# Half-array units in pairs, PSUM banks handed out by modelled free time, late loads on GpSimd, in a fused spectral filter and gated MLP

## The chip, the cores and the metric

The kernel runs on one core of one Trainium2 chip. The metric is the device time of one execution in microseconds (us), lower is better. A core has TensorE (PE, matrix products), VectorE (DVE), ScalarE (ACT), GpSimd (POOL) and SyncE (SP, which here only issues DMAs). PSUM, into which TensorE writes, is used as eight banks of 512 float32 columns on 128 partitions.

## The reference

```python
def _A_ref(x, w_r, w_i):                 # x: 1 x 2048 x 512
    X = jnp.fft.rfft2(x.astype(jnp.float32), axes=(-2, -1))
    X = X * (w_r + 1j * w_i)             # weights 2048 x 257
    return jnp.fft.irfft2(X, s=(S, D), axes=(-2, -1)).astype(jnp.bfloat16)

def _B_ref(x, w_gate, w_up, w_down):     # 512 x 1792, 512 x 1792, 1792 x 512
    h = _gelu(x @ w_gate) * (x @ w_up)
    return h @ w_down

x = A_x
xn = _layernorm(x, axis=-1)
return x + _A_ref(xn, A_w_r, A_w_i) + _B_ref(xn, B_w_gate, B_w_up, B_w_down)
```

Two branches work on the same normalised rows: a two-dimensional Fourier transform with a filter and its inverse, and a gated MLP. Both are added to the input.

## The kernel before

**The MLP branch** is the backbone. The 2048 rows are four blocks b of 512. For each of 14 chunks fc of the hidden width, `gate` multiplies (four matmuls of 512 columns), ScalarE applies gelu into one of two `gl` buffers, `up` multiplies (four matmuls), and VectorE multiplies the two into `hT`. A `down` for one tile of 128 rows is 14 matmuls over all chunks, in three parts of 5, 5 and 4. The downs of a block stand among the gates and ups of the next block, after fc 2, 5, 8 and 11; the last block's four downs come at the end.

**The Fourier branch** runs as small units between these. In the forward part, `trans` transposes normalised rows into `xnT`, `butter` folds them on VectorE, `unit_D(j)` transforms along the width for row tile j (16 of them) into `xs`, and `unit_A(j)` does the first stage along the sequence into `tt`. Each `tt` tile is stored to a scratch tensor in HBM and loaded back in another order as `tv`. `load_tv(j - 1)` is issued right behind the store of tile j. `unit_B(h)` needs all 16 `tv` loads; it does the second stage, and VectorE multiplies by the filter (`mul`, four operations with `Wr` and `Wi`) into `yy`. `unit_C(h)` begins the inverse; its results go through a second scratch tensor and come back as `vv`, laid in the arena that held the forward constants. `unit_row`, which needs all of `vv`, `unit_E(j)` and `unit_F(j)` finish the inverse; the last sum is stored to the output.

D, E, F, gate, up and down use the whole 128 x 128 array. A, B and C use half of it per matmul: A and C contract over 64 partitions, two row halves side by side, and B writes 64 output partitions, two column halves side by side. Each has four matmuls of about 257 columns.

**The order** is written by hand. After each gate, each up and each part of a down stands a `hook`, numbered from 0; `at(h, ...)` puts units at hook h. Block 0 has hooks 0 to 27 and each later block 40, because of its downs. Work that `mul` and the final sums leave for VectorE waits in `later` until the next `flush`: at a hook after an up or a part of a down it is flushed at that hook, and at a hook after a gate it waits until the up's product has been issued. TensorE takes all of it in this order.

**Banks** are fixed: gate 0, up 1 and 2 in turn, D and E 3 and 4, A, C (a pair of banks) and F 5 and 6, B 3 and 4, trans and down 7.

**Queues.** The first loads (x, the MLP weights, the forward constants) are issued by SP and ScalarE at the start. The late loads (`wd` at hooks 10 to 16, `be` at 18, four loads of `Wr` and `Wi` at 19 to 28, `cm` at 31 and 34, `gm` at 52) are issued by SP through `load_late`, each with a wait for the TensorE work before its hook. SP also issues all scratch stores and loads in program order. GpSimd computes `rstd` for each chunk of four row tiles (chunks 1 to 3 at hooks 3, 13 and 23; the normalisation that needs it is three and four hooks later), and copies one row per E unit.

**The start.** `warm(24)` runs 24 matmuls on a zeroed tile `dumm` to get TensorE going. ScalarE writes one column of the same `dumm` with a gelu, which loads its table.

The class `_Prog` records every operation with the keys it reads and writes and derives the semaphore waits. Lines of use in the profile: 283 is every ordinary DMA, 287 a late load, 305 the first gelu, 324 the warm-up, 330 to 342 the normalisation, 351 trans, 391 to 394 D, 415 and 419 A, 425 the eviction to `tt`, 439 B, 445 its eviction, 451 to 454 the filter's products, 465 C, 471 its eviction, 484 the row, 498 E, 524 to 527 F, 559 gate, 562 gelu, 572 up, 575 the product `hT`, 585 down, 596 the sum behind a down.

Of the kernel before, what the change touches and what calls it, by code (L numbers as in the profile page):

```python
# [7 lines left out]
ACT = mybir.ActivationFunctionType  # L8
# [3 lines left out]
F32 = mybir.dt.float32  # L12
# [5 lines left out]
P = 128  # L18
# [91 lines left out]
class _Prog:  # L110
# [17 lines left out]
    def op(self, eng, fn, r=(), w=(), dma=False, after=()):  # L128
        deps = [(ev, True) for ev in after]
        for k in r:  # L130
            if k in self.writer:
                deps.append((self.writer[k], True))
        for k in w:
            if k in self.writer:
                deps.append((self.writer[k], False))
            for ev in self.readers.get(k, ()):
                deps.append((ev, False))
        need = {}
        for (st, val), raw in deps:
            if st == eng and not dma and (eng == "pe" or not raw):  # L140
                continue
            need[st] = max(need.get(st, 0), val)
        known = self.known[eng]
        need = {s: v for s, v in need.items() if known.get(s, 0) < v}
        need = {s: v for s, v in need.items()
                if not any(s2 != s and self.clk[(s2, v2)].get(s, 0) >= v for s2, v2 in need.items())}
        for s, v in need.items():
            for a, b in self.clk[(s, v)].items():
                if known.get(a, 0) < b:
                    known[a] = b  # L150
        if dma:
            st = next((d for d in self.dsem if known.get(d, 0) >= self.cnt[d]), None)
            if st is None:
                st = "d%d" % len(self.dsem)
                self.sem[st] = self.es.enter_context(self.nc.semaphore("s_" + st))
                self.cnt[st] = 0
                self.dsem.append(st)
# [33 lines left out]
def bass_parallel_sum__spectral_gfnet__glu_gated_geglu__prompt_kernel(  # L191
# [26 lines left out]
    with ExitStack() as es:  # L218
# [46 lines left out]
        mhalf = sb("mhalf", [P, 4], F32)  # L265
        rstd = sb("rstd", [P, NJ], F32)
        dumm = sb("dumm", [P, 512], F16)

        psum = es.enter_context(nc.psum_tensor("ps", [P, 8 * 512], F32))
        psum_h = psum[:, :].bitcast(F16)  # L270
# [8 lines left out]
            return psum[:, i * 512:(i + 2) * 512].rearrange("p (a c) -> p a c", a=2)[:, :, 0:KD]  # L279


        def dma(eng, dst, src, r=(), w=()):
            return op(eng, lambda e: e.dma_start(dst, src), r=r, w=w, dma=True)  # L283

        def load_late(dst, src, keys):

            op("sp", lambda e: e.dma_start(dst, src), w=keys, dma=True, after=[("pe", pr.cnt["pe"])])
# [17 lines left out]
        op("act", lambda e: e.activation(dumm[:, 0:1], mhalf[:, 0:1], ACT.Gelu_apprx_tanh), r=["mhalf"], w=["dumm"])  # L305
        dma("sp", fd[:], c_fd.ap(), w=["fd"])
        load_w(wg_sb, wgv, "wg", 2, 6, "sp")
        load_w(wu_sb, wuv, "wu", 2, 6, "sp")
# [33 lines left out]
            op("dve", lambda e: e.tensor_scalar(xn[:, j % 4, :], x_sb[:, j, :], ag[:, j, 0:1], rstd[:, j:j + 1], ALU.subtract, ALU.mult),  # L342
               r=[("x", j, 0), ("x", j, 1), ("ag", j), ("rstd", j)], w=[("xn", j % 4)])

        def trans(m, dcs, jjs, bk, eng="dve"):
            def f(e):
                ins = None
                for a, dc in enumerate(dcs):
                    for c, jj in enumerate(jjs):
                        i = a * len(jjs) + c  # L350
                        ins = e.transpose(bank_h(bk)[:, i * P:(i + 1) * P], xn[:, jj, dc * P:(dc + 1) * P], ident[:])  # L351
# [28 lines left out]
        later = []  # L380

        def unit_D(j):
            bk = 3 + j % 2
            m = j // 4
            f = fold[m % 2]
            k = ("fold", m % 2)
# [20 lines left out]
                w=[("vv", h)] + (AKEYS if h == 0 else []))  # L407

        def unit_A(j):
            bk = 5  # L410
            x4 = xs[j % 4]

            def fn(e):
# [16 lines left out]
                load_tv(j)  # L430

        def unit_B(h):
            bk = 3

            def fn(e):
                ins = None
# [18 lines left out]
            later.append(mul)  # L455

        def unit_C(h):
            bk = 5
            y = yy[h % 4]

            def fn(e):
# [18 lines left out]

        def unit_row():

            bk = 3
            op("pe", lambda e: e.matmul(bank(bk)[0:32, 0:64], vv[:, :, 256], EMs[:, 0:64], start=True, stop=True,
                                        skip_group_check=True), r=["be"] + VALL, w=[("ps", bk)])
            op("act", lambda e: e.activation(row[:], bank(bk)[0:32, 0:64], ACT.Copy, scale=SC_E), r=[("ps", bk)], w=["row"])
# [1 line left out]
                r=["row"], w=["z256"] + [("xn", i) for i in range(4)])  # L488

        def unit_E(j):  # L490
            bk = 3 + j % 2

            def fn(e):
                o = bank(bk).rearrange("p (c r b q) -> p c b r q", c=2, r=2, b=2)
# [22 lines left out]
                dma("sp", ov[b, :, j, :], osb[k][64 * b:64 * b + 64, :], r=[("osb", k)], w=[("out", j, b)])  # L517

        def unit_F(j):
            bk = 5 + j % 2  # L520

            def fn(e):
                z = zt[j % NZ]
# [27 lines left out]

        def gate(b, fc):
            k = gun[0]
            bg = 0

            def fn(e):
                ins = None
# [18 lines left out]

        def down(b, jj):
            j = 4 * b + jj
            bk = 7

            def part(f0, f1):
                def fn(e):
                    ins = None
                    for fc in range(f0, f1):
                        ins = e.matmul(bank(bk), hT[b % 2][:, fc, jj * P:(jj + 1) * P], wd_sb[:, fc, :], start=(fc == 0), stop=(fc == NFC - 1))  # L585
# [5 lines left out]
            part(5, 10)  # L591
            hook()
            part(10, 14)

            def add(dst, key):
                op("dve", lambda e: e.tensor_tensor(dst, bank(bk), x_sb[:, j, :], ALU.add), r=[("ps", bk), ("acc", j), ("x", j, 0), ("x", j, 1)], w=[key])  # L596
# [37 lines left out]
        for m in range(1, 4):  # L634
# [6 lines left out]
            at(a + 8, (trans, m, (0, 1), (0, 1, 2, 3), 7))  # L641
            at(a + 9, (trans, m, (2, 3), (0, 1, 2, 3), 7))
# [12 lines left out]
        for j in range(NJ):  # L655
            at(101 + 3 * j, (unit_E, j))
# [8 lines left out]
            ln_norm(2 * i)  # L665
            ln_norm(2 * i + 1)
        for i in range(2):
            trans(0, (0, 1), (2 * i, 2 * i + 1), 3 + 2 * i, "dve")
            trans(0, (2, 3), (2 * i, 2 * i + 1), 4 + 2 * i, "act")
        for b in range(4):  # L670
            for fc in range(NFC):
                gate(b, fc)
# [60 lines left out]
```

## Time and profile before

| what | us |
|---|---|
| median of 3 runs | 230.37 (229.06 to 230.85) |
| the profiled execution | 228.33 |
| its span, first to last instruction | 226.5 |
| TensorE busy | 198.8 (88%) |
| VectorE busy | 113.2 (50%) |
| ScalarE busy | 89.4 (39%) |
| GpSimd busy | 9.3 (4%) |
| first gate starts | 14.26 |
| first unit of stage B starts | 87.36 |
| the row unit starts | 154.57 |
| last down ends, about | 222.7 |

In the profile's busy slices one digit stands for one fortieth of the span, 5.66 us, and gives the busy share in tenths. In a timeline row stand start, duration, engine, line and operation; rows of several instructions are merged and end with the count, and the bracket says how long the engine had been idle and what ended that. In the chain of work that ended last, a row has start, duration and what it was. In a list of waits stand the engine and line that waited, what it waited for, the total, the number of times and the longest. In a row of the costliest groups stand the count, then the busy time in us and the mean duration in ns. A row of DMA issues has the count, the size of each and the median us from issue to landing.

### The profile page before, as it was taken

Reading aid. Unit: us, or ns where it says so; the run is one execution under the profiler, and the core shown is the slowest. Engines: PE = TensorE matmul, PEld = TensorE weight load, DVE = VectorE, ACT = ScalarE, POOL = GpSimd, SP = SyncE. Lnnn points to the kernel's source line nnn. Section 1 sums busy time; section 2 is a strip of 40 time slices with the busy share of each in tenths; the row PEclk is TensorE's granted clock in tenths of the full one; section 3 lists DMA queues with packets and bytes.
Section 4 is the critical chain, followed back from the end, with each engine's and each line's share of the span. In section 5 each row is a group of like instructions: output and inputs, shape, how many; then the busy total and the mean of one; then the engine's idle time right before and its main releaser. Section 6 shows DMA issues by size and latency. Waiting matters only on the chain.

```text
span 226.5 us, 3103 instructions
## 1 busy us (share of the span) xinstructions
PE 198.8 (88%) x1145; PEld 89.4 (39%) x1145; DVE 113.2 (50%) x262; ACT 89.4 (39%) x157; POOL 9.3 (4%) x26
## 2 busy tenths in 40 slices
PE   1989898999976805999999999997999999999883
PEld 0344444445422302333333333333555555555331
DVE  3568795978211201646556566631464555555311
ACT  2025454655325201444454545341654544544100
POOL 0201010010000000000000000000100101101000
PEclk9999999999997965999999999999999999999998
DMA  6999869799995640042231322330011102101011
GB/s 162 266 308 319 239 164 225 181 157 151 142 135 142 171 108 23 21 98 76 64 90 55 93 70 70 81 84 1 19 33 45 46 23 49 33 15 26 23 31 38
DMA packets 23887, 23.09 MB, mean 102 GB/s; under 512 B 1984, under 2 KB 22464, under 8 KB 23488
## 3 DMA queue, kind: packets, MB, share of 16 engines
q1 hardware_dynamic: 23104, 22.10, 43.0%
q10 hardware_dynamic: 768, 0.79, 1.4%
q8 instruction: 9, 0.15, 0.3%
q14 instruction: 6, 0.05, 0.1%
HBM read 16.57 MB, written 6.31 MB: 101 GB/s over the span
## 4 chain that ended last, share of the span: by engine, by line
PE 74%; DMA 16%; DVE 3%; ACT 2%; ACTq 1%; issue 1%; SPq 1%
PE ps L585 19%; PE ps L572 19%; PE ps L559 18%; DMA scr<-tt 12%; PE ps L324 3%; PE ps L439 3%; PE ps L465 2%; PE ps L498 2%; DMA tv<-scr 2%; PE ps L351 1%; DMA arena<-scr 1%; DVE osb L596 1%; DMA scr<-vp 1%; ACTq L283 1%; PE ps L415 1%; DVE hT L575 1%
## 5 line engine op out<-in xcount | busy, mean ns | idle before, releaser
L575 DVE TENSOR_TENSOR hT<-ps,gl 128x512 bf16<-128x512 f32 x56 | 38.6, 690 | 54.8 <-PE ps L572 43.1
L559 PE MATMUL ps<-xnT,wg 128*128 128x512 f16 x224 | 58.5, 384 | 4.6 <-ACT gl L562 3.7
L572 PE MATMUL ps<-xnT,wu 128*128 128x512 f16 x224 | 59.5, 389 | 0.0
L585 PE MATMUL ps<-wd,hT 128*128 128x512 bf16 x224 | 53.7, 381 | 1.9 <-DVE osb L596 1.9
L562 ACT ACTIVATE gl<-ps 128x512 bf16<-128x512 f32 x56 | 33.4, 597 | 41.3 <-PE ps L559 37.7
L559 PEld LDWEIGHTS ps<-xnT,wg 128*128 128x128 bf16 x224 | 20.5, 99 | 28.1 <-ACT gl L562 5.2
L585 PEld LDWEIGHTS ps<-wd,hT 128*128 128x128 bf16 x224 | 20.6, 98 | 26.5 <-issue 3.5
L572 PEld LDWEIGHTS ps<-xnT,wu 128*128 128x128 bf16 x224 | 20.9, 100 | 23.2 <-issue 4.9
L445 ACT ACTIVATE xc<-ps 128x514 f16<-128x514 f32 x16 | 9.6, 600 | 19.3 <-PE ps L439 19.3
L596 DVE TENSOR_TENSOR x_sb<-ps,x_sb 128x512 bf16<-128x512 f32 x11 | 7.6, 692 | 18.3 <-PE ps L585 18.3
L425 ACT ACTIVATE tt<-ps 128x514 f16<-128x514 f32 x16 | 9.6, 598 | 16.8 <-PE ps L419 9.2
L439 PE MATMUL ps<-tv,be 128*64 128x257 f16 x64 | 6.8, 294 | 8.7 <-DMA tv<-scr 8.7
L505 ACT ACTIVATE zt<-ps 128x512 bf16<-128x512 f32 x16 | 9.5, 595 | 9.9 <-PE ps L498 9.9
L532 ACT ACTIVATE eo<-ps 128x512 bf16<-128x512 f32 x16 | 9.5, 595 | 9.2 <-PE ps L527 9.2
L471 ACT ACTIVATE vp<-ps 128x514 bf16<-128x514 f32 x16 | 9.6, 598 | 7.3 <-PE ps L465 7.3
L330 DVE BATCH_NORM_STATS2 st<-x_sb 128x6 f32<-128x512 bf16 x16 | 10.6, 684 | 3.0 <-DMA x_sb<-in_A_x_dram 3.0
L324 PE MATMUL ps<-dumm 128*128 128x512 f16 x24 | 7.8, 500 | 4.8 <-ACT dumm L305 4.8
L398 ACT ACTIVATE xs<-ps 128x512 f16<-128x512 f32 x16 | 9.6, 597 | 4.3 <-PE ps L394 4.3
L506 POOL COPY zt<-xn 1x128 bf16<-1x128 bf16 x16 | 4.5, 283 | 155.5 <-ACT zt L505 155.5
L537 DVE TENSOR_TENSOR ys<-eo 128x256 bf16<-128x256 bf16 x16 | 4.6, 289 | 9.3 <-ACT eo L532 9.3
L596 DVE TENSOR_TENSOR osb<-ps,x_sb 128x512 bf16<-128x512 f32 x5 | 3.5, 691 | 10.3 <-PE ps L585 10.3
L439 PEld LDWEIGHTS ps<-tv,be 128*64 128x64 f16 x64 | 2.3, 110 | 15.5 <-issue 12.9
(59 smaller groups left out, 154.4 us busy)
## 6 DMA issues: line engine op xcount, KB each, us to landing
scr<-tt SPq DMA_DIRECT2D x16, 128.5 KB
tv<-scr SPq DMA_DIRECT2D x16, 128.5 KB
scr<-vp SPq DMA_DIRECT2D x16, 128.5 KB
arena<-scr SPq DMA_DIRECT2D x16, 128.5 KB
out_dram<-osb SPq DMA_DIRECT2D x32, 64.0 KB
wg<-in_B_w_gate_dram SPq DMA_DIRECT2D x3, 512.0 KB, 10.0
wu<-in_B_w_up_dram SPq DMA_DIRECT2D x3, 512.0 KB
x_sb<-in_A_x_dram SPq DMA_DIRECT2D x5, 256.0 KB, 13.5
```

The source lines that it names most:

```text
L324: ins = e.matmul(bank(7), dumm[:, 0:128], dumm[:], start=True, stop=True)
L330: op("dve", lambda e: e.bn_stats(st[:, j, :], x_sb[:, j, :]), r=[("x", j, 0), ("x", j, 1)], w=[("st", j)])
L398: op("act", lambda e: e.activation(x4[:].rearrange("p (a c r) -> p a c r", a=2, r=4), bank(bk).rearrange("p (a r c) -> p a c r", a=2, r=4) ...
L425: op("act", lambda e: e.activation(t4[:], pair(bk), ACT.Copy, scale=SC_A), r=[("ps", bk), ("ps", bk + 1)], w=[("tt", j % 4)])
L439: ins = e.matmul(bank(bk + ri)[64 * hh:64 * hh + 64, 0:257], be[:, 64 * ri:64 * ri + 64], tv[:, 16 * hh + h, :], start=True, stop=True, sk ...
L445: op("act", lambda e: e.activation(xc[s2][:, :, 0:KD], pair(bk), ACT.Copy, scale=SC_B), r=[("ps", bk), ("ps", bk + 1)], w=[("xc", s2)])
L559: ins = e.matmul(bank(bg), wg_sb[:, dc, fc * P:(fc + 1) * P], xnT[:, dc, b * 512:(b + 1) * 512], start=(dc == 0), stop=(dc == 3))
L562: op("act", lambda e: e.activation(gl[k % 2][:], bank(bg), ACT.Gelu_apprx_tanh), r=[("ps", bg)], w=[("gl", k % 2)])
L572: ins = e.matmul(bank(bu), wu_sb[:, dc, fc * P:(fc + 1) * P], xnT[:, dc, b * 512:(b + 1) * 512], start=(dc == 0), stop=(dc == 3))
L575: op("dve", lambda e: e.tensor_tensor(hT[b % 2][:, fc, :], bank(bu), gl[k % 2][:], ALU.mult), r=[("ps", bu), ("gl", k % 2)], w=[("hT", b % ...
L585: ins = e.matmul(bank(bk), hT[b % 2][:, fc, jj * P:(jj + 1) * P], wd_sb[:, fc, :], start=(fc == 0), stop=(fc == NFC - 1))
L596: op("dve", lambda e: e.tensor_tensor(dst, bank(bk), x_sb[:, j, :], ALU.add), r=[("ps", bk), ("acc", j), ("x", j, 0), ("x", j, 1)], w=[key])
```

## The change

- The first gelu on ScalarE writes a tile of its own, `warm_o`, and not `dumm`.
- Banks are no longer fixed. A function `take` keeps a model of TensorE's time (`pt`) and for each bank the time at which it should come free. It gives each unit the bank, or the pair of neighbouring banks, that is free first. A down holds its bank until its last part.
- The late loads are issued by GpSimd, with the same wait for TensorE. A DMA from GpSimd gets a semaphore of its own.
- The D units stand at earlier hooks, each block of four from the first hook after its fold: 4, 6, 8, 10, 12 and so on to 36, where they stood 2.5 hooks apart up to 41.
- A units run in pairs, two hooks after the second D of a pair (last pair at hook 38; the last A stood at 43).
- B and C units run in pairs: B(i), B(i+1) at hook 46 + 3i and C(i), C(i+1) at 51 + 3i, for even i. C(i) stood at 50 + 3i.

```diff
-            st = next((d for d in self.dsem if known.get(d, 0) >= self.cnt[d]), None)
+
+            st = None if eng == "pool" else next((d for d in self.dsem if known.get(d, 0) >= self.cnt[d]), None)
...
+        pt = [0.0]
+        free = [0.0] * 8
+
+        def take(n, dur, hold):
+            i = min(range(9 - n), key=lambda i: max(free[i:i + n]))
+            pt[0] += dur
+            for k in range(i, i + n):
+                free[k] = pt[0] + hold
+            return i
...
         def load_late(dst, src, keys):
 
-            op("sp", lambda e: e.dma_start(dst, src), w=keys, dma=True, after=[("pe", pr.cnt["pe"])])
+            op("pool", lambda e: e.dma_start(dst, src), w=keys, dma=True, after=[("pe", pr.cnt["pe"])])
...
-        op("act", lambda e: e.activation(dumm[:, 0:1], mhalf[:, 0:1], ACT.Gelu_apprx_tanh), r=["mhalf"], w=["dumm"])
+        op("act", lambda e: e.activation(warm_o[:], mhalf[:, 0:1], ACT.Gelu_apprx_tanh), r=["mhalf"], w=["warm_o"])
...
         def unit_A(j):
-            bk = 5
+            bk = take(2, 0.3, 1.6)
...
         def gate(b, fc):
-            bg = 0
+            bg = take(1, 0.87, 1.2)
...
-            bu = 1 + k % 2
+            bu = take(1, 0.87, 1.8)
...
         def down(b, jj):
-            bk = 7
+            bk = take(1, 0.0, 1e9)
...
+                pt[0] += 0.217 * (f1 - f0)
...
             part(10, 14)
+            free[bk] = pt[0] + 1.2
...
         for j in range(NJ):
-            h = 4 + j * 2.5
+            h = (4, 6, 8, 10, 12, 14, 17, 19, 22, 24, 27, 29, 32, 33, 34, 36)[j]
             at(h, (unit_D, j))
-            at(h + 2, (unit_A, j))
-        for i in range(16):
-            at(46 + 3 * i, (unit_B, i))
-            at(50 + 3 * i, (unit_C, i))
+            if j % 2:
+                at(h + 2, (unit_A, j - 1), (unit_A, j))
+        for i in range(0, 16, 2):
+            at(46 + 3 * i, (unit_B, i), (unit_B, i + 1))
+            at(51 + 3 * i, (unit_C, i), (unit_C, i + 1))
```

The other units take banks in the same way: trans, D, E, F and the row one bank each, B and C two.

More of the change, by code (lines that the diff above doesn't have):

```diff
@@ L267, in bass_parallel_sum__spectral_gfnet__glu_gated_geglu__prompt_kernel @@
         dumm = sb("dumm", [P, 512], F16)
+        warm_o = sb("warm_o", [P, 1], F32)
         psum = es.enter_context(nc.psum_tensor("ps", [P, 8 * 512], F32))
@@ L343, in ln_norm, with trans @@
                r=[("x", j, 0), ("x", j, 1), ("ag", j), ("rstd", j)], w=[("xn", j % 4)])
-        def trans(m, dcs, jjs, bk, eng="dve"):
+        def trans(m, dcs, jjs, eng="dve"):
+            bk = take(1, 0.45, 1.2)
             def f(e):
@@ L382, in unit_D @@
         def unit_D(j):
-            bk = 3 + j % 2
+            bk = take(1, 0.33, 1.2)
             m = j // 4
@@ L432, in unit_B @@
         def unit_B(h):
-            bk = 3
+            bk = take(2, 0.3, 1.6)
             def fn(e):
@@ L457, in unit_C @@
         def unit_C(h):
-            bk = 5
+            bk = take(2, 0.3, 1.6)
             y = yy[h % 4]
@@ L481, in unit_row @@
         def unit_row():
-            bk = 3
+            bk = take(1, 0.1, 1.0)
             op("pe", lambda e: e.matmul(bank(bk)[0:32, 0:64], vv[:, :, 256], EMs[:, 0:64], start=True, stop=True,
@@ L490, in unit_E @@
         def unit_E(j):
-            bk = 3 + j % 2
+            bk = take(1, 0.22, 1.2)
             def fn(e):
@@ L519, in unit_F @@
         def unit_F(j):
-            bk = 5 + j % 2
+            bk = take(1, 0.44, 1.2)
             def fn(e):
@@ L640, in bass_parallel_sum__spectral_gfnet__glu_gated_geglu__prompt_kernel @@
                 at(a + 6 + i // 2, (ln_norm, 4 * m + i))
-            at(a + 8, (trans, m, (0, 1), (0, 1, 2, 3), 7))
-            at(a + 9, (trans, m, (2, 3), (0, 1, 2, 3), 7))
+            at(a + 8, (trans, m, (0, 1), (0, 1, 2, 3)))
+            at(a + 9, (trans, m, (2, 3), (0, 1, 2, 3)))
             at(a + 10, (butter, m, 0))
@@ L667, in bass_parallel_sum__spectral_gfnet__glu_gated_geglu__prompt_kernel @@
         for i in range(2):
-            trans(0, (0, 1), (2 * i, 2 * i + 1), 3 + 2 * i, "dve")
-            trans(0, (2, 3), (2 * i, 2 * i + 1), 4 + 2 * i, "act")
+            trans(0, (0, 1), (2 * i, 2 * i + 1), "dve")
+            trans(0, (2, 3), (2 * i, 2 * i + 1), "act")
         for b in range(4):
```

5 lines of the change are left out of this document (3 added, 2 removed).

## The prediction

> **What bounds the kernel now.** I read the page first (busy slices, then each engine's share of the chain that ended last), then TensorE's list of waits, then windows.
>
> ```profile
> PE   1989898999976805999999999997999999999883
> ...
> DMA  6999869799995640042231322330011102101011
> ...
> PE 74%; DMA 16%; DVE 3%; ACT 2%; ACTq 1%; issue 1%; SPq 1%
> ```
>
> TensorE is at 8 or 9 in nearly every slice; the hole is in slices 12 to 15 (about 66 to 90 us, 5.66 us each), after a run of slices in which the DMA engines are full. The chain gives DMA the second share, 16%. So there are two bounds: DMA up to the start of stage B, TensorE from there on. What ended TensorE's idle time, and one wait of ScalarE behind it (total us, times, longest):
>
> ```profile
> ACT tt L425 <- DMA scr<-tt: 7.6, 3, 4.9
> ...
> PE ps L439 <- DMA tv<-scr: 8.7, 1, 8.7
> PE ps L324 <- ACT dumm L305: 4.8, 1, 4.8
> PE ps L559 <- ACT gl L562: 3.7, 1, 3.7
> PE ps L484 <- DMA arena<-scr: 2.2, 1, 2.2
> PE ps L585 <- DVE osb L596: 1.9, 3, 0.8
> ```
>
> 8.7 is B(0) waiting for the last tv load, 4.8 the warm-up waiting for ScalarE, 2.2 the row unit waiting for the last vv load, 1.9 the last downs sharing bank 7. The 3.7 is put on gelu, but gelu stood behind an eviction to tt that waited for an older tt store: that is DMA again.
>
> ```profile
> 26.00:87.36 61.36, 47.79 (x303) 21.90 (x299) 29.35 (x61) 24.79 (x44) 2.01 (x2) 0.92 0.81 154
> 46.00:68.00 22.00, 19.75 (x130) 9.10 (x127) 9.90 (x23) 9.00 (x17) 1.01 (x1) 1.00 1.14 147
> ```
>
> The last columns are granted clock, DMA share and GB/s. From 26 us, when the first loads have landed, to B(0) at 87.36 the DMA engines do 0.81 x 61.4 = 49.7 us of work. At the share of the full stretch, 1.14, that takes 43.6 us and could end at 69.6: some 18 us are lost to transfers that weren't there to be started.
>
> **The change part by part.** *The warm-up gets its own tile.*
>
> ```profile
> 0.86 0.27 DVE L295 MEMSET dumm<- 128x256 uint32 x1 [0.86 <-PEq L718]
> ...
> 4.78 7.76 PE L324 MATMUL ps<-dumm 128*128 128x512 f16 x24 [4.78 <-ACT dumm L305]
> ...
> 8.33 0.73 DVE L342 TENSOR_SCALAR xn<-x_sb,ag,rstd 128x512 f16<-128x512 bf16 x2 [0.27 <-POOL rstd L338]
> ...
> 12.38 1.06 PE L351 MATMUL ps<-ident,xn 128*128 128x128 f16 x16
> ```
>
> The 24 matmuls then wait for the memset alone (done at 1.13), start at about 1.2 and end at 9.0; xn is complete at 9.06. The transposes start at 9.0 instead of 12.38: everything behind them is **3.4 us earlier** (bounds 0, if the weights were late, and 3.4). It counts through the next part only.
>
> *Forward stage: D and A earlier, A in pairs, late loads on GpSimd.* A hook is a place after a gate, an up or a part of a down. A(15) moves from hook 43 to hook 38; B(0) stays at 46.
>
> ```profile
> 51.68 10.73 DMA scr<-tt
> ...
> 79.63 4.17 DMA scr<-tt
> 83.81 3.42 DMA tv<-scr
> 87.36 0.64 PE ps L439 x4
> 88.00 1.82 PE ps L572 x4
> ...
> 92.50 0.34 PE ps L439 x4
> 92.84 0.97 PE ps L559 x4
> 93.81 0.33 PE ps L465 x4
> 94.14 0.97 PE ps L572 x4
> ...
> 102.48 0.86 PE ps L572 x4
> ...
> 207.75 3.04 PE ps L585 x14
> ```
>
> ```profile
> 63.69 0.28 PE L415 MATMUL ps<-xs,arena 64*128 64x257 f16 x2
> ```
>
> This last row is A(13), which stood at hook 38 and had met no long stall. After the change hook 38 comes 3.4 earlier, 1.5 earlier for seven pairs (0.22 each, next part), and 0.7 later for D(14) and D(15), now in front of it: 59.5. From there to B(0) stand one A pair (0.65), five gates or ups at 0.86 and one down of 3.04: TensorE could start B(0) at **67.5**. The data: the pair ends near 60.1, ScalarE evicts two tt tiles (0.60 each) and, at worst, a gelu before them, so the last store is issued at about 61.5. In the run before, from the last store's issue (79.63) to B(0) it took 7.73 (4.17 + 3.42 and issue). That gives 69.2. If the store stands in a loaded queue as at 51.68 (10.73), it is 75.8. The bounds are thus 67.5 and 75.8; I take **70**, near the unloaded row, since the last late load ahead of B is issued at hook 34 and the DMA work above could be done at 69.6.
>
> The loads on GpSimd: SP loses twelve issues and their waits for TensorE, so a store no longer stands behind a 514 KB load in SP's queue.
>
> ```profile
> 42.86 0.71 SPq L287 DMA_DIRECT2D Wr<-in_A_w_r_dram  x1
> ```
>
> ```profile
> Wi<-in_A_w_i_dram SPq DMA_DIRECT2D x2, 514.0 KB, 11.4
> ...
> cm<-c_cm SPq DMA_DIRECT2D x2, 512.0 KB, 8.0
> ```
>
> ```profile
> L338 POOL TENSOR_TENSOR rstd<-vpe,mhalf 128x4 f32<-128x4 f32 x3 | 3.0, 1007 | 36.3 <-DVE vpe L337 36.3
> ...
> L334 DVE BATCH_NORM_AGGREGATE ag<-st 128x2 f32<-128x6 f32 x16 | 1.7, 158 | 0.0
> ```
>
> No DMA issued by GpSimd is in this trace. On SP an issue took 0.71 and the landing 11.4; GpSimd could be held for as little as the one or as long as the other. Behind it in GpSimd's queue stands rstd of the next chunk (hooks 13 and 23, behind loads of hooks 12 and 22); VectorE's xn waits for rstd, TensorE's transposes for xn. Aggregate and xn are three hooks apart, about 3.5 us; four aggregates (0.16 each), an addition and rstd (1.01) fill 1.8 of it, so the slack is some 1.7. Nearer to the issue row than to the landing, I take about 3 us, 1.3 over the slack: B(0) at **71**. The gain of this stage: 87.36 - 71 = **16.4**. TensorE still stands about 3.5 us before B(0), which dropped the clock before (up 1.82 instead of 0.86 behind it), so I count no gain of clock there.
>
> The Trainium skill, *DMA: Bandwidth & Descriptors*, section "Issuing engines are not separate DMA queues", speaks against this step: all issuers share 16 engines, and a second one saves issue time alone. The sum by it is the first rival. Its *SBUF — State Buffer*, "Who interferes with whom", adds that GpSimd's descriptor writing is blocked during some VectorE instructions; no row here shows it, and the sum doesn't use it.
>
> *Pairs of B and C (and A).* In the rows at 92.50 a half-array unit takes 0.34 and the full-array matmuls behind it 0.97, not 0.86: 0.11 to come back. Of the 0.34, four matmuls of 257 columns, two at a time at 0.86/4 x 257/512 = 0.108 each, are 0.216; so 0.12 to go in. Side by side, two units spare one entry and one return, 0.23. Sixteen pairs of B and C: **3.8** (bounds 0, if the second unit waits for its banks, and 3.8). The eight A pairs lie before B(0) and are in the 70.
>
> What a pair makes late:
>
> ```profile
> 97.20 0.43 DVE L451 TENSOR_TENSOR m_0<-xc,Wr 128x514 bf16<-128x514 f16 x1 [1.37 <-ACT xc L445]
> ...
> 98.22 0.29 DVE L454 TENSOR_TENSOR yy<-m_0 128x257 bf16<-128x257 bf16 x1
> ```
>
> One unit's products hold VectorE 1.31, a pair's 2.6, with hT products queued behind, whose ends free ups' banks and gelu's two buffers. C comes five hooks later, four matmul blocks or more (3.5 to 4.8): where the flush puts hT ahead (hooks 46 and 64) that is a tie. I take **1.0 lost** over the stage (bounds 0 and 8 x 0.9 = 7).
>
> *Banks by modelled free time.* Following the hand-out through the hooks with its own durations, the shortest reuse is 1.47 us after the former user (a bank of a C, taken by a B); an eviction takes 0.60. Nothing gained or lost in mid-kernel. At the end:
>
> ```profile
> 211.56 3.21 PE ps L585 x14
> 214.79 0.70 DVE osb L596
> 215.54 3.21 PE ps L585 x14
> ```
>
> A last down comes every 3.98 us instead of 3.04. With its own bank each, two intervals give 0.94 each and the first, which had F(15) to fill it, 0.5: **2.4** (bounds 1.9, the wait alone, and 2.4).
>
> *C ends at hook 93 instead of 95*, 1.9 us more ahead of the row unit, less 0.5 for the second eviction: of the 2.2 wait **1.4** goes (bounds 0 and 2.2).
>
> **Sum**, against the profiled execution of 228.33 (span 226.5 and 1.83 around it): 228.33 - 16.4 - 3.8 + 1.0 - 2.4 - 1.4 = 205.3. The median of the runs shown, 230.37, is 2.0 above that execution; the forecast for a median is **207**.
>
> **The rivals.**
> - *The DMA engines bound the stage, whatever the queue.* For: share 1.14 in the full stretch. Against: 0.81 over the whole. At a share of 1.0 the 49.7 us end at 75.7; the last tv load may then be last of all, and 3.42 more makes B(0) 79. Time: 207 + 8 = **215**. The Trainium skill's section on issuing engines, above, amounts to this.
> - *GpSimd's queue becomes the bound.* If a load holds it for the landing time, rstd of two chunks is late by about 8 each; B(0) is near 87 and only the later gains stay: **222**. For: rstd stands behind loads. Against: SP's 0.71.
> - *Pairs save nothing*, because each unit pays for itself even beside its like, or the second waits: 207 + 3.8 = **211**.
> - *Slower: late loads starve B and C.* From hook 19 (about 31 us) four W loads (514 KB) and two of cm (512 KB) have to bring 3.1 MB, in time for C(0) near 75. The whole gain is gone if they end at 98 or later, a rate under 3.1 MB / 67 us = 46 GB/s, a third of the 147 of the full stretch. At 40 GB/s they end at 108: **240**. For: no row prices GpSimd's DMAs. Against: hooks of slack.
>
> **How the numbers follow.** Forecast 0.58 (own range 201 to 212: B(0) at 67.5 to 74, clock kept or not, burst 0 to 3), pairs without saving 0.10, DMA engines 0.19, GpSimd's queue 0.08, starved loads 0.05. The range leaves out the last two and the ends of the forecast: **200 to 218**. Runs of before differ by 0.8%, so 1% is about what can be told from no change: faster 0.92, same 0.03, slower 0.05.
>
> **What would show it.** Warm-up at 1.2, first gate near 11; A(15) near 60; B(0) between 67 and 76, with a single wait for tv under 8.7; GpSimd's queue with loads, xn's wait for rstd in VectorE's list; a second B or C about 0.22 behind the first, and one 0.97 block per pair; the last downs 3.04 apart. I am wrong if B(0) is after 80, or if new waits for hT or for banks appear between B(0) and the row unit.

## The result, and the profile after

The changed kernel is faster: 221.58 us (median of 4, 219.57 to 222.46) against 230.61 for the kernel before on the same chip, a ratio of 0.960 with a 95% interval of 0.950 to 0.969. The forecast was 207, with a range of 200 to 218: right in sign, more than twice too large in size, and outside its range. The profiled execution took 219.57, which is 8.8 less than the 228.33 of before; the sum had 23.0. A time below is the median of a kernel's runs, and a ratio is to the kernel before on the same chip. Ratios leave disturbed, slower runs out, but the traces of e3, e5, e10 and e12 come from such runs, so a difference that one of these traces alone shows is weak evidence.

The busy slices and the chain's shares of the changed kernel, on its page:

```profile
PE   7798899899449947999999999959999999999992
PEclk9999999999976996999999999996999999999999
DMA  5999988999875540133323234220011111001011
...
PE 61%; DMA 24%; DVE 7%; ACT 2%; issue 2%; POOL 1%; SPq 1%; ACTq 0%
```

A slice is 5.45 us here. TensorE's hole did not close, it moved forward: it was at about 66 to 90 us, now it is two holes, at about 54 to 65 and 76 to 82 us (digits of 4), and at each the granted clock falls to 6 or 7 tenths. A third drop stands near 147 us. DMA has 24% of the chain; it had 16%. By stretches, cut at the first unit of B and at the row unit (us; the last stretch includes what lies around the span):

| | before | forecast | after | the late loads of W and cm left out |
|---|---|---|---|---|
| up to B(0) | 87.4 | 71.0 | 82.9 | 71.9 |
| B(0) to the row unit | 67.2 | 63.0 | 63.7 | 62.5 |
| the row unit to the end | 73.8 | 71.4 | 73.0 | 71.3 |
| the profiled execution | 228.3 | 205.3 | 219.6 | 205.7 |

The last column is an experiment told below. It is what the forecast described, to within a microsecond in each stretch; the kernel as changed is 11 us later at B(0). So 11.9 of the 14.3 us by which the sum missed the profiled execution are one term, what the late loads do to the transfers of the forward stage; the other 2.3 lie behind B(0).

TensorE's waits after (total us, times, longest), and one each of ScalarE's and VectorE's from the list of all engines. Lines of after: 430 is A, 440 its eviction to `tt`, 413 the eviction of D to `xs`, 454 B, 499 the row, 574 gate, 587 up, 600 down, 613 the sum behind a down:

```profile
ACT tt L440 <- DMA scr<-tt: 14.7, 4, 6.0
...
DVE xn L356 <- POOL rstd L352: 1.1, 4, 0.5
```

```profile
PE ps L454 <- DMA tv<-scr: 4.2, 1, 4.2
...
PE ps L430 <- ACT xs L413: 3.2, 1, 3.2
PE ps L600 <- ACT tt L440: 3.1, 1, 3.1
PE ps L499 <- DMA arena<-scr: 2.7, 1, 2.7
```

The wait of B(0) went from 8.7 to 4.2: TensorE is ready for B(0) at 78.7, as in the kernel before, and `tv` is complete 4.5 earlier. The forecast had TensorE ready at 67.5. Two waits on ScalarE, 3.2 and 3.1, stand where there was one of 3.7, and both have ScalarE's first row behind them: it waited 14.7 us in all (7.6 before) for older stores of `tt` before it could overwrite one of the four buffers. An A's eviction that waits holds the evictions and gelus queued behind it, and with them TensorE. The chain of work that ended last shows the stores (start, duration, what it was):

```profile
48.23 14.90 DMA scr<-tt
...
76.48 3.23 DMA scr<-tt
79.73 3.01 DMA tv<-scr
82.88 1.07 PE ps L454 x8
83.95 1.82 PE ps L587 x4
...
91.25 0.56 PE ps L454 x8
```

A small store took 14.90 us at 48.23, and 3.23 at 76.48, with the late loads done. The timeline (start, duration, engine, line, the idle time before and what ended it) has the two dates that matter in front of this chain, and a late load on GpSimd:

```profile
10.53 1.02 PE L574 MATMUL ps<-xnT,wg 128*128 128x512 f16 x4 [0.78 <-ACT xnT L378]
...
70.65 0.28 PE L430 MATMUL ps<-xs,arena 64*128 64x257 f16 x2
...
35.90 0.84 POOL L301 DMA_DIRECT2D Wr<-in_A_w_r_dram  x1 [1.15 <-PE ps L587]
```

The first gate is 3.7 earlier than before. The last A pair, at hook 38, starts at 70.65; the prediction put it at 59.5. Windows give the state of the DMA engines (window, length, five engines' busy time, clock, DMA share, GB/s):

```profile
26.00:58.00 32.00, 26.93 (x192) 13.71 (x190) 22.17 (x50) 14.76 (x27) 8.84 (x11) 1.00 0.97 190
58.00:70.00 12.00, 8.61 (x35) 3.51 (x35) 1.38 (x2) 4.35 (x9) 0.56 (x1) 0.72 0.64 162
```

Up to 58 the DMA share is 0.97 (the kernel before had 1.14 from 46 to 68, so 0.97 need not be the most). From 58 to 70 it is 0.64, and TensorE stands for 3.4 us of 12 and has 0.72 of its clock: neither is saturated, and the stage waits for stores that land late.

### The profile page after: what moved, and what is told of

The parts are those of the page before. It is cut to its first block, busy times and chain, and to the rows that moved or that the text cites. A ratio compares the mean times of both kernels' runs of the same rounds, so it can differ in the third digit from the quotient of the medians.

```text
span 217.8 us, 3082 instructions
## 1 busy us (share of the span) xinstructions
PE 194.6 (89%) x1131; PEld 94.2 (43%) x1145; DVE 112.2 (52%) x262; ACT 88.1 (40%) x157; POOL 18.3 (8%) x38
## 3 DMA queue, kind: packets, MB, share of 16 engines
q0 software_dynamic: 1488, 5.32, 12.0%
## 4 chain that ended last, share of the span: by engine, by line
PE 61%; DMA 24%; DVE 7%; ACT 2%; issue 2%; POOL 1%; SPq 1%; ACTq 0%
PE ps L600 20%; DMA scr<-tt 16%; PE ps L587 15%; PE ps L574 14%; DMA tv<-scr 3%; DVE st L344 3%; PE ps L454 2%; PE ps L480 2%; DVE hT L590 2%; PE ps L513 2%; DMA scr<-vp 2%; DMA x_sb<-in_A_x_dram 2%; DMA arena<-scr 1%; ACT tt L440 1%; DVE xn L356 1%
## 5 line engine op out<-in xcount | busy, mean ns | idle before, releaser
L587 PE MATMUL ps<-xnT,wu 128*128 128x512 f16 x224 | 58.4, 384 | 0.0
L600 PEld LDWEIGHTS ps<-wd,hT 128*128 128x128 bf16 x224 | 21.9, 101 | 28.4 <-issue 7.6
L574 PEld LDWEIGHTS ps<-xnT,wg 128*128 128x128 bf16 x224 | 21.3, 99 | 24.2 <-issue 4.1
L440 ACT ACTIVATE tt<-ps 128x514 f16<-128x514 f32 x16 | 9.2, 602 | 17.0 <-DMA scr<-tt 14.7
L486 ACT ACTIVATE vp<-ps 128x514 bf16<-128x514 f32 x16 | 8.7, 598 | 10.9 <-PE ps L480 10.9
L344 DVE BATCH_NORM_STATS2 st<-x_sb 128x6 f32<-128x512 bf16 x16 | 10.6, 684 | 3.4 <-DMA x_sb<-in_A_x_dram 3.4
L460 ACT ACTIVATE xc<-ps 128x514 f16<-128x514 f32 x16 | 8.7, 600 | 5.9 <-PE ps L454 5.9
L454 PE MATMUL ps<-tv,be 128*64 128x257 f16 x64 | 5.5, 297 | 4.2 <-DMA tv<-scr 4.2
L338 PE MATMUL ps<-dumm 128*128 128x512 f16 x24 | 6.9, 456 | 1.2 <-DVE dumm L309 1.2
L430 PE MATMUL ps<-xs,arena 64*128 64x257 f16 x32 | 4.2, 280 | 3.3 <-ACT xs L413 3.2
```

Source lines behind the costliest of these rows:

```text
L344: op("dve", lambda e: e.bn_stats(st[:, j, :], x_sb[:, j, :]), r=[("x", j, 0), ("x", j, 1)], w=[("st", j)])
L440: op("act", lambda e: e.activation(t4[:], pair(bk), ACT.Copy, scale=SC_A), r=[("ps", bk), ("ps", bk + 1)], w=[("tt", j % 4)])
L454: ins = e.matmul(bank(bk + ri)[64 * hh:64 * hh + 64, 0:257], be[:, 64 * ri:64 * ri + 64], tv[:, 16 * hh + h, :], start=True, stop=True, sk ...
L574: ins = e.matmul(bank(bg), wg_sb[:, dc, fc * P:(fc + 1) * P], xnT[:, dc, b * 512:(b + 1) * 512], start=(dc == 0), stop=(dc == 3))
L587: ins = e.matmul(bank(bu), wu_sb[:, dc, fc * P:(fc + 1) * P], xnT[:, dc, b * 512:(b + 1) * 512], start=(dc == 0), stop=(dc == 3))
```

## The experiments

The theories at the start: **pile-up** (M in the expectations): the late loads, once they go out without delay, stand beside the `tt` stores, and the stores land late whatever queue the loads are in; against it **packets** (P): the many small packets of GpSimd's queue take turns with the store's few, so that another queue or another shape would free the stores. The expectations name two more: D (the DMA engines bound the stage, whatever the queue) and S (SP's own order, in which a `tv` load that waits for its store holds up the next store). Later ones ask which of the store's delay, SP's order and TensorE's place in the order decides B(0).

**Which engine issues the loads.**

```diff
-            op("pool", lambda e: e.dma_start(dst, src), ...
+            op("sp", lambda e: e.dma_start(dst, src), ...      # e1_loads_sp
+            op("act", lambda e: e.dma_start(dst, src), ...     # e2_loads_act
```

> The changed kernel with one part undone: the late loads are issued by SP again. Theory P (packets): in the changed kernel the tt stores, in small packets on SP's queue, take turns with GpSimd's packets of about 3.6 KB (1488 packets for 5.32 MB) and get about an eighth of the bytes, so that a store took 14 to 15 us; on SP each load waits its turn between stores, a store takes at most some 10 us, and stage B starts at 76 to 80 against 82.9; time 214 to 219. Rival M (pile-up): it is the load's freedom from SP's waits that lets them pile up, whatever their packets; the same here as P. Rival D (the DMA engines bound the stage whatever the queue): B at 82 to 84, time within 1% of the changed kernel, 220 to 223.

> The changed kernel with the late loads issued by ScalarE: a queue of its own beside SP's, as free of SP's waits as GpSimd's, but with a packet for each row (514 B for Wr and Wi) instead of 3.6 KB. P: stores get about half of the bytes; none takes over 8 us, B starts at 70 to 74, time 207 to 212. M: the loads pile up just the same, stores still take 14 to 15 us, B at 82 to 83, time 220 to 223. D: as M in time, with a DMA share near 1.1 up to B.

On SP: 227.4, ratio 0.985 (0.979 to 0.991). No theory had that: the changed kernel without its GpSimd part is 6 us slower. SP's own timeline, TensorE's row for B(0), the window, and SP's longest wait up to B(0):

```profile
47.02 0.71 SPq L301 DMA_DIRECT2D Wr<-in_A_w_r_dram  x1
...
91.55 1.07 PE L454 MATMUL ps<-tv,be 128*64 128x257 f16 x8 [8.57 <-DMA tv<-scr]
```

```profile
26.00:58.00 32.00, 30.32 (x214) 15.28 (x212) 23.63 (x53) 17.62 (x32) 2.01 (x2) 1.00 0.64 154
```

```profile
SPq L297 <- DMA scr<-tt: 39.5, 9, 6.9
```

The first load of Wr goes out at 47.02 where GpSimd issued it at 35.90; the DMA engines are at 0.64 and not 0.97 up to 58. In SP's queue a late load stands behind the `tv` loads, and these wait for their stores to land: 39.5 us in nine waits. SP's waits for ScalarE's evictions (3.9) and, in front of late loads, for TensorE (3.0) are small beside that. The prediction's first rival, that the engines bound the stage whatever the queue, does not hold: only the queue differs here, and the kernel is 6 us slower. The Trainium skill (*DMA: Bandwidth & Descriptors*, "Issuing engines are not separate DMA queues") says that a second issuer saves little more than issue time. This run doesn't decide on that rule: the eleven late loads ahead of B(0) took SP 6.9 us to issue, about as much as the gain.

On ScalarE: 220.6, ratio 0.959 (0.951 to 0.968), the same as on GpSimd. The chain and the queue of these loads (packets, MB, share), then GpSimd's queue of the changed kernel:

```profile
46.70 11.46 DMA scr<-tt
...
82.76 1.07 PE ps L454 x8
```

```profile
q10 hardware_dynamic: 7360, 6.10, 15.5%
```

```profile
q0 software_dynamic: 1488, 5.32, 12.0%
```

With a queue of quite other packets (7,360, first loads included, against 1,488) a store still takes 11.46, and B(0) starts at 82.76 against 82.88. Packets fall; pile-up stands. It also shows that what matters is leaving SP, and not which engine takes over. D wanted a DMA share near 1.1 up to B(0): it is 1.11 from 26 to 58, but 0.71 to 70 and 0.43 from there on, so the engines do not bound the end of the stage.

**What the late loads cost.** Two ways to leave out the four loads of W and the two of cm (3.1 MB). In e3 GpSimd fills the three tiles with zeros at hook 24. In e8 no tile is filled: the filter's products read rows of `x_sb` as W, and C reads part of `xnT` as cm, with instructions of the same shapes.

```diff
-                at(19 + 3 * (2 * hh + i), (load_late, t[...], v[hh], ...))
-            at(31 + 3 * i, (load_late, cm[...], cmv[...], ...))
+            at(24, (zero, t[:], ...)); at(24, (zero, cm[:], ...))   # e3 alone: e.memset(dst, 0.0) on GpSimd
...
-            wr_b = Wr[:, h:h + 1, 0:KD].to_broadcast([P, 2, KD])
+            wr_b = x_sb[:, h:h + 1, 0:KD].to_broadcast([P, 2, KD])  # e8; wi_b alike, cm from a view of xnT
```

> The changed kernel without the loads of Wr, Wi and cm (GpSimd writes zeros into them once instead), so that the filter and the inverse work on zeros; 3.1 MB less to move before B. P and M: stores take 3 to 5 us, B starts at 68 to 70, TensorE waits for it under 2 us, time 206 to 209. D: 3.1 MB less at 150 GB/s is 20 us of DMA work, so the same. A fourth theory, S (SP's own order: a load of tv waits for its store in front of the next store, whatever else runs): B at 76 or later, time 213 or more.

> The changed kernel without the loads of Wr, Wi and cm: the filter and the inverse read other tiles that are there (x_sb and xnT) in their place, so nothing is written instead. M (the stores are slow because loads are under way beside them): a store takes 3 to 5 us all through, TensorE doesn't wait for ScalarE at an A or a down before B, B starts at 68 to 72, time 206 to 211. S (SP's own order): stores wait behind tv loads whatever else runs; B at 76 or later, time 213 or more. D (DMA work): as M.

e3: 215.2, ratio 0.932 (0.925 to 0.938), where 206 to 209 was expected, but it cannot be read as the price of the loads: B(0) is at 83.69 in its trace. VectorE's and GpSimd's timeline:

```profile
33.37 0.80 DVE L359 TENSOR_SCALAR xn<-x_sb,ag,rstd 128x512 f16<-128x512 bf16 x2 [0.18 <-POOL rstd L355]
...
46.60 3.53 POOL L300 MEMSET Wr<- 128x4128 bf16 x1
...
46.66 10.86 DVE L359 TENSOR_SCALAR xn<-x_sb,ag,rstd 128x512 f16<-128x512 bf16 x2 [0.18 <-POOL rstd L355]
```

The two VectorE instructions that take 0.80 elsewhere took 10.86 while GpSimd's three memsets ran (3.5 us each): the experiment put a stall of its own in. e8 has no such stall: 205.3, ratio 0.891 (0.884 to 0.898). Its chain and its queue:

```profile
64.27 3.91 DMA scr<-tt
68.19 3.60 DMA tv<-scr
71.93 0.63 PE ps L455 x8
```

```profile
q0 software_dynamic: 624, 2.16, 3.6%
```

The last store takes 3.91, the last A pair starts at 61.86 where the forecast had 59.5, and B(0) at 71.93 where it had 71. The six loads alone are thus worth 11 us to B(0) and 16 us (221.6 to 205.3, by the ratios 0.069 of 230) to the kernel, part of it the clock, which is 1.00 throughout here and 0.969 on average after. Their own work: 12.0% of 217.8 is 26.1 us of 16 engines, 3.6% of 203.9 is 7.3; so 18.8 us for 3.16 MB, 168 GB/s, against some 295 for the other late loads.

**Where between the store and B(0) it is lost.** e4 issues a `tv` load three stores later, so that SP does not stand waiting for the store it has just issued. e9 adds four buffers for `tt` (tiles of `vp`, unused until then), so that ScalarE need not wait. e11 leaves the queue and puts B, C, row, E and F eight hooks later instead. e10 has all three.

```diff
-            if j > 0:
-                load_tv(j - 1)
+            if j > 2:
+                load_tv(j - 3)                       # e4, e9, e10; the last three at j = 15
-            t4 = tt[j % 4]
+            t4 = tt[j % 4] if j % 8 < 4 else vp[j % 4][:].bitcast(F16)   # e9, e10
-            at(46 + 3 * i, (unit_B, i), (unit_B, i + 1))
-            at(51 + 3 * i, (unit_C, i), (unit_C, i + 1))
+            at(54 + 3 * i, (unit_B, i), (unit_B, i + 1))   # e10, e11; row 108, E 109 + 3j, F 113 + 3j
+            at(59 + 3 * i, (unit_C, i), (unit_C, i + 1))
```

> The changed kernel with the tv load of tile j issued three stores later instead of one, so that four stores may be under way and none waits behind a load that waits for the store before it. S: the stores' chain goes at TensorE's pace, B starts at 70 to 73, time 208 to 212. P: the stores beside the piled-up loads stay slow (8 us or more at 42 to 60 us), but the eight stores behind them run faster than the 2.1 us each that they took; B at 75 to 79, time 213 to 218. D: no change, B at 82 to 83.

> The kernel with tv loads three stores later, and eight tt tiles instead of four (the four vp tiles, idle in this stage, serve as the others). Its forerunner with four (214.6) had TensorE wait 1.9 and 5.0 for tt and xs. If these waits come from too few tiles, they go, A(15) is at 60 to 63, and what is left is a wait of B(0) for tv. If DMA work then bounds, B(0) stays at 77 to 80 with that wait 5 us or more and the time 212 to 215; if the tiles were the bound, B(0) is at 72 to 74 and the time 207 to 210.

> The changed kernel with only that shift of eight hooks. D and S together: the waits of TensorE at A for ScalarE stay (6 us), the wait of B(0) for tv (4.2) goes, the row unit waits less than 2.7; time 214 to 217. If the forward waits only grow by what B's wait loses: 220 to 222.

> tv loads three stores later and eight tt tiles, and all of B, C, the row unit, E and F eight hooks later (B(i) at 54 + 3i, C(i) at 59 + 3i, the row at 108, E and F from 109 and 113), so that TensorE does the gates, ups and a down of eight hooks before B instead of waiting. D (the DMA engines bring the last tv at 79.7 whatever TensorE does): B(0) at 79 to 81 again, but now reached by TensorE at about 77, a wait under 3 us, no dropped clock; time 205 to 209. Rival: what is moved ahead of B is missing later (the row unit and E come too late for the end): 213 or more.

| | time | ratio | B(0), its wait for tv |
|---|---|---|---|
| after | 221.6 | 0.960 (0.950 to 0.969) | 82.88, 4.2 |
| e4, later tv loads | 214.6 | 0.929 (0.923 to 0.935) | 79.44, 0.2 |
| e9, and eight buffers | 217.7 | 0.940 (0.932 to 0.948) | 79.79, 10.5 |
| e11, later B alone | 213.6 | 0.930 (0.922 to 0.938) | 87.00, none |
| e10, all three | 212.2 | 0.916 (0.909 to 0.923) | 83.96, 5.9 |

The timeline of e9, and its chain:

```profile
61.36 0.27 PE L434 MATMUL ps<-xs,arena 64*128 64x255 f16 x2
...
79.79 1.07 PE L456 MATMUL ps<-tv,be 128*64 128x257 f16 x8 [10.49 <-DMA tv<-scr]
```

```profile
54.69 15.44 DMA scr<-tt
...
70.76 4.79 DMA scr<-vp
75.57 4.09 DMA tv<-scr
```

e4 takes 7 us from the kernel with one change. Its profiled execution is 5.2 shorter than that of the changed kernel: 3.4 up to B(0), which starts without a wait, and 1.7 from there to the row unit, where the granted clock is 1.00 and not 0.97. In e9 TensorE meets no long wait on the way, and the last A pair ends near 61.8, where the prediction had 60.1. And yet `tv` is complete at 79.8, as in e4: the place of A in the order does not decide it, the landing of the stores and SP's queue behind them do. The store at 54.69 takes 15.44; the last two tiles are evicted by 62.8, but the last store is issued at 70.76, behind a `tv` load that waits for the late one. In place of several smaller waits TensorE has one of 10.5, and the kernel is no faster than e4 (212 to 215 was expected).

So of the 11 us, 7.5 (71.9 to 79.4) are still there in e4, and 3.4 went with the later `tv` loads. This split is a difference of single traces and rough: with the same forward stage as the changed kernel (82.88), B(0) stood at 85.81 in e14 and 87.54 in e5. Nor are the 7.5 landing alone, since a late store still holds up SP's queue; no run gives stores and `tv` loads a queue each. e10 was expected at 205 to 209 and missed it (its runs go from 209.98 to 214.53); in its trace the last store and load took 4.76 and 5.80, where they took 3.23 and 3.01 in the changed kernel.

**A shorter landing.** In e12 the tiles Wr and Wi have rows of 257 columns and not 258, so that a load's destination has no gap of one element between its rows. e13 is e10 with this.

```diff
-        Wr = sb("Wr", [P, 16, 258], BF16)
+        Wr = sb("Wr", [P, 16, KD], BF16)
```

> The changed kernel with Wr and Wi laid 257 columns wide instead of 258, so that what a partition gets is one run of 8224 B in both memories. The late loads' queue took 12.0% of 16 engines' span here and 3.6% without W and cm: 18.8 us for 3.16 MB, 168 GB/s, against 295 GB/s for the rest. If that is due to the 514 B rows of W, the queue's share falls to 8 or 9%, the stores beside it wait less, B(0) is at 77 to 80 and the time 214 to 218. If rows don't matter: B at 82 to 83.5, 220 to 223; then 514 B rows that start on odd places can also make VectorE's products slower (430 ns each before).

> The three together: tv loads three stores later with eight tt tiles, the shift of eight hooks, and W 257 wide. If both the rows and the shift count, TensorE no longer waits before the row unit, and the time is 201 to 205; if the rows don't matter, as with the first two alone, 205 to 209.

DMA issues of after (count, KB, median us from issue to landing), then of e12 with its queue:

```profile
Wr<-in_A_w_r_dram POOLq DMA_DIRECT2D x2, 514.0 KB, 10.9
...
Wi<-in_A_w_i_dram POOLq DMA_DIRECT2D x2, 514.0 KB, 13.4
```

```profile
Wr<-in_A_w_r_dram POOLq DMA_DIRECT2D x2, 514.0 KB, 6.9
...
Wi<-in_A_w_i_dram POOLq DMA_DIRECT2D x2, 514.0 KB, 8.5
```

```profile
q0 software_dynamic: 1232, 5.32, 10.4%
```

The same bytes land in 6.9 and 8.5 us, and VectorE's products with Wr take about 426 ns in both kernels. In e13 they land in 8.2 and 10.2, against 10.6 and 13.4 in e10. e12 takes 216.7, ratio 0.942 (0.936 to 0.948), as expected, but in its trace B(0) is at 83.45 and not at the expected 77 to 80, and the queue's share is 10.4% and not 8 or 9; where its gain arises, that trace does not show. e13 takes **205.3, ratio 0.893 (0.888 to 0.898)**, 1.7 under the forecast with all loads in place, and the best version that ran. TensorE's row of e13's slices and its longest wait:

```profile
PE   7988989899999999999999999976999999999990
```

```profile
PE ps L501 <- DMA arena<-scr: 3.1, 1, 3.1
```

The holes between 54 and 82 are gone: B(0) starts at 76.41 in the timeline, without a wait, because gates and ups now fill the time until `tv` is there.

**The pairs and the warm-up by themselves.** e5 is the changed kernel with B and C one by one; e6 is the kernel before with `warm_o` alone.

```diff
-        for i in range(0, 16, 2):
-            at(46 + 3 * i, (unit_B, i), (unit_B, i + 1))
-            at(51 + 3 * i, (unit_C, i), (unit_C, i + 1))
+        for i in range(16):
+            at(46 + 3 * i, (unit_B, i))
+            at(50 + 3 * i, (unit_C, i))
```

> The changed kernel with B and C one by one, at the hooks of the kernel before (B(i) at 46 + 3i, C(i) at 50 + 3i). If a pair spares one entry and one return of the half array, 0.23 each as in the prediction, sixteen pairs are worth 3.7 between B(0) and the row unit, and the time is 224.5 to 226. Rival: pairs save nothing because what they spare comes back as waits for VectorE's products; 221 to 222.5.

> The kernel before with the warm-up's own tile and nothing else. The first gate starts 3.4 to 3.8 us earlier in any case. If the DMA stage bounds the start of B, B(0) stays at 86.5 to 88 and the time within 1% of before (229 to 232); TensorE's waits before B grow by as much as the start is earlier. Rival: the earlier start carries through; B(0) near 84, time 226 to 228.

e5: 225.9, ratio 0.971 (0.961 to 0.981). Its timeline:

```profile
87.54 0.64 PE L454 MATMUL ps<-tv,be 128*64 128x257 f16 x4 [8.03 <-DMA tv<-scr]
...
155.01 0.21 PE L499 MATMUL ps<-be,arena 128*32 128x64 f16 x1 [2.53 <-DMA arena<-scr]
```

From B(0) to the row unit it takes 67.5, the changed kernel 63.7: the pairs are worth 3.8 there. Other traces agree: 67.2 in the kernel before and 68.2 in e6, both with single units, 63.4 in e1 and 64.1 in e2, both with pairs. By the whole time it is less sure, 0.971 against 0.960, as the intervals overlap. In e5's trace B(0) itself is 4.7 later than in the changed kernel, though nothing in front of it was changed. e6: 230.1, ratio 0.994 (0.989 to 0.999). B(0):

```profile
87.87 0.64 PE L440 MATMUL ps<-tv,be 128*64 128x257 f16 x4 [7.68 <-DMA tv<-scr]
```

The warm-up alone moves the first gate (10.57 against 14.26) and nothing at B(0) (87.87 against 87.36): what comes earlier in front is waited away on the way there. What the prediction said of it, that its 3.4 us count through the next part only, holds.

**The row unit.** SP issues the `vv` load of unit h - 1 behind the store of unit h. e14 puts two loads behind both stores of a pair, one pair later; e15 does the same in e13.

```diff
-            if h > 0:
-                load_vv(h - 1)
+            if h % 2 and h > 1:
+                load_vv(h - 3); load_vv(h - 2)      # the last two at h = 15
```

> The changed kernel with the vv loads of a pair of C issued behind both stores of the next pair, so that the second store of a pair doesn't stand behind a load that waits. In the changed kernel the last store was issued at 139.65, some 0.8 us after its tile was ready, took 3.59, and the row unit waited 2.66; behind that wait the granted clock had dropped and a part of a down took 3.45 instead of 2.1. If SP's order makes the wait: last store 0.7 us earlier, row wait 1.6 to 2.0, perhaps no dropped clock; time 218 to 221. Rival: the stores' and loads' own landing makes it (3.6 and 3.2); wait 2.4 to 3 as before, time 220 to 222.5.

> The fastest version so far (205.3: tv loads three stores later, eight tt tiles, B to F eight hooks later, W 257 wide), with the same order of the vv loads. Its only long wait of TensorE is the row unit's 3.1. If SP's order makes it: 203 to 205; if the landing does: 205 to 206.

e14: 223.3, ratio 0.965 (0.958 to 0.971); e15: 206.3, ratio 0.895 (0.890 to 0.899). No gain in either, and both lie above what was expected of the landing alone (up to 222.5 and 206). The chain of after, then of e14:

```profile
139.65 3.59 DMA scr<-vp
...
143.25 3.18 DMA arena<-scr
```

```profile
142.91 3.02 DMA scr<-vp
...
145.95 5.33 DMA arena<-scr
```

Store and load one after the other take 6.8 us in the one and 8.4 in the other (5.7 in the kernel before); the wait is the way out and back of the last C, not SP's order.

## Why the prediction was right or wrong

- **The warm-up: right.** It starts at 1.19 and the first gate at 10.53, 3.7 earlier, for 3.4 in the sum.
- **GpSimd's queue as a bound: wrong in the harmless direction.** An issue took 0.84 at 35.90, near SP's 0.71, and `xn` waited for `rstd` 1.1 us in all, 0.5 at most (1.4 and 0.5 in the kernel before); the 1.3 charged for it is not found in TensorE's waits.
- **"hook 38 ... 59.5": the step that failed.** It took A(13) at 63.69 in the run before, saw no long stall up to there and subtracted. The same late loads came later in that run, since SP held them back: the first load of Wr went out at 42.86 there and at 47.02 in e1. Issued by GpSimd it goes out at 35.90, and the loads pile up on the stores *before* hook 38. The price of a loaded store (10.73, quoted there) was charged to the last store alone, as a bound; it fell on those in the middle, at 14.9, and came back by `tt`'s four buffers to ScalarE and TensorE: 70.65, where e8, without those loads, has 61.86. From hook 38 to B(0) it was again near the forecast, 12.2 us for 11.5: two evictions, then 3.23 + 3.01 from the last store to B(0), but with SP's last stores 2.0 to 2.3 us apart, each behind a wait for the one before. The prediction's own sign of being wrong, B(0) after 80, came.
- **"the last late load ahead of B is issued at hook 34, and the DMA work above could be done at 69.6"** was the reason for 70. The engines were indeed busy, 0.97 up to 58, but B needs the *last* store and load, and those go out one behind the other after the bytes are done. That the loads' work ends in time does not say that small transfers beside it do.
- **The rivals.** The first put B(0) at 79 and the time at 215. Its number is that of e4 and e9 (79.4 and 79.8; 214.6 and 217.7), in which `tv` loads follow their stores later, but its mechanism, engines full to 75.7, is not: from 58 to 70 the share is 0.76 in e4 and 0.82 in e9, and from there to B(0) 0.47 in both. That the number fits is luck. GpSimd's queue, pairs that save nothing, and starved B and C did not come.
- **The pairs: right.** 0.56 for the pair at 91.25 and 3.8 by e5, as forecast (sixteen times its 0.23 is 3.7); the 1.0 charged for bursts is not seen, since e5 gives the pairs' worth with it included.
- **The row unit: wrong in sign, small.** 1.4 of 2.2 was to go; 2.66 is there. C's end came earlier on TensorE, but the last store and load took 6.8, and 5.7 before. The wait also cost more than itself. The timelines of after and before:

```profile
146.57 0.21 PE L499 MATMUL ps<-be,arena 128*32 128x64 f16 x1 [2.66 <-DMA arena<-scr]
...
148.37 3.45 PE L600 MATMUL ps<-wd,hT 128*128 128x512 bf16 x9
```

```profile
156.03 2.10 PE L585 MATMUL ps<-wd,hT 128*128 128x512 bf16 x9
```

 The second fence is the kernel before: the nine matmuls behind the row unit took 2.10 there and 3.45 after, at a dropped clock. The length of the wait alone does not say whether it drops (last section).
- **The last downs: right, and hidden in the total.** Their sums follow each other at 3.02, from the timeline of VectorE:

```profile
210.97 0.69 DVE L613 TENSOR_TENSOR osb<-ps,x_sb 128x512 bf16<-128x512 f32 x1 [2.33 <-PE ps L600]
213.99 0.69 DVE L613 TENSOR_TENSOR osb<-ps,x_sb 128x512 bf16<-128x512 f32 x1 [2.33 <-PE ps L600]
```

 The forecast was 3.04. Of the 2.4 us that this brings, the last stretch shows 0.8, since the dropped clock behind the row unit took the rest; e8, whose clock held there, has 71.3 where the forecast had 71.4.

What stays open: why a store beside these loads takes 11 to 20 us (20.02 in the chain of e4, 11.46 in e2) (bytes in front of it on the same engines would explain it, but no run shows where a store's packets wait); why B(0) lies up to 4.7 us apart in traces with the same forward stage; and how the 7.5 us are shared between late stores and the queue behind them.

## What to carry to other kernels

Freeing a queue lets large transfers out earlier: look at which small, dependent transfers are then under way beside them, and charge the loaded price to every one of these, buffers and in-order waits included, not to the last alone. On a queue that waits in order, let a load follow its store by several places. If the landing can't be shortened, fill its time: moving the consumer eight hooks back was worth as much as mending the queue, and the two together with eight buffers and a gap-free destination reached the forecast.

## What the runs showed of the hardware

- A load into rows of 257 of 258 elements took 10.9 and 13.4 us to land where one into full rows took 6.9 and 8.5 in e12 (8.2 and 10.2 in e13, 6.9 and 7.4 in e15), and 1,488 packets became 1,232.
- In e3, two VectorE instructions took 10.86 us in place of 0.80 while three GpSimd memsets of 3.5 us ran.
- The clock behind the row unit's wait, in the sixteen profiled executions with it (waits of 2.2 to 3.4 us): in six the four microseconds behind it had a granted clock of 0.57 to 0.67 (waits of 2.49 in e4, 2.62 in e1, 2.66 after, 2.96 in e3, 3.06 in e13, 3.42 in e15), in ten it stayed at 1.00 (2.22 before, 2.49 in e12, 3.00 in e8, 3.29 in e14 among them). The length alone does not decide. The Trainium skill, *TensorE: Matmul & The Clock Gate*, "What's actually happening", has a window of about 3.4 us that runs freely, whatever the kernel does, and an idle one throttles: that the outcome changes for waits of one length agrees with the first; that waits of 2.49 to 3.06, shorter than the window, can drop the clock does not agree with a window that has to be idle throughout. No run here shows the window itself.
